# Reordering TensorE's opening work in a fused attention and MoE kernel: transposes of a block ahead of the value products, up products between them

## The chip, the cores and the metric

The kernel runs on one core of a Trainium2 chip. The metric is the device time of one launch in microseconds (us). A profiled run also gives the span, from the first to the last instruction of the core; it is some 1.7 us shorter than the launch's time. Before the change the time was 303.53 us (median of three runs, 303.49 to 303.58). The profiled run was a fourth one: its time was 303.82 us and its span 302.1 us. Some executions fall into a slower state, with a lower granted TensorE clock and a longer time. Comparisons rest on runs of the fast state, which have a mean granted clock of 0.99 to 1.00; where a median in a table includes a slow run, the median of the fast runs stands beside it.

Names used throughout: PE is TensorE, ACT is ScalarE, DVE is VectorE, POOL is GpSimd, SP is the engine that issues most transfers.

## The reference

For each of 8 batches and 8 heads, 576 positions of 64 elements attend to the 64 positions up to their own. The outputs, laid out as 4608 tokens of 512 elements, go through an MLP of width 2048 with a gated activation.

```python
scores = scale * q @ k.T            # window of 64, causal
attn   = softmax(where(mask, scores, -1e9))
x      = (attn @ v)  # -> (4608, 512)
h = x @ w_in
g = h * sigmoid(1.702 * h)
out = g @ w_out
```

## The kernel before

The whole schedule is written by hand: a list of calls, each of which emits instructions to in-order engines. The tokens are cut into 36 blocks of 128. A block m passes through `scores(m)`, `exp(m)`, `pv(m)` (value products), `norm(m)`, `x_mm(m)` (four PE transposes) and `x_out(m)` (a copy to SBUF by ACT). Four blocks are a chunk, and a chunk goes through up products (`up_mm`), a tanh (`up_th`), a gate (`up_g`) and down products. The parts that matter here:

```python
ps pools: psS 1 x 2 banks, psT 1 x 2 banks, psH 2 banks, psO 2 banks   # all of PSUM
# ... cut ...
def pv(m):                       # 16 products on PE; the Tacc pool has ONE buffer
    acc = T_of[m] = psT.tile([P, 2, 512], fp32, name="Tacc", tag="T")
    ...
def norm(m):                     # DVE: reciprocal of the sums, then xs = Tacc * rc
    ...
def x_mm(m, pool, tag):          # PE: four transposes of xs to PSUM
    ...
def x_out(m):                    # ACT: copy into xT of the chunk
    nc.scalar.copy(out=x_dst(m), in_=X_of.pop(m)[:])

def x_dma(m):                    # blocks 16 and up: a transposing transfer instead, issued by SP
    nc.sync.dma_start_transpose(out=x_dst(m), in_=xs_of.pop(m))

def load_bf16(b, i):             # POOL: three casting loads (q, k, v) of one piece of a batch
    for w, src in enumerate((q, k)):
        nc.gpsimd.dma_start(out=heads(rows[b % 2][w][0:n, i, :]), in_=rows_of(src, b, i))
    nc.gpsimd.dma_start(out=v_nat[b % 2][0:n, i, :, 0:D], in_=rows_of(v, b, i))
# ... cut: the opening, as it stands before the change ...
    x_mm(0, psO, "O")
    x_out(0)
    scores(3, masked=True)
    exp(3, masked=True)
    cast_v(0, 3, nc.vector, parts=(1,))
    pv(2)
    norm(2)
    x_mm(1, psO, "O")
    x_out(1)
    warm(3)
    UU['0.0.0'] = up_mm(0, 0, 4, 0, 128, wide=True)
```

"up 0.4.128" is the up unit of chunk 0 whose first column group is 4 and whose tokens start at 128. An up unit is 16 products of 128 columns. `warm` are idle products that keep PE busy. The values v of a piece reach `v_nat` and `v_off` through casts on POOL, in that engine's order, once their load has landed.

The softmax here doesn't subtract the row's maximum and nothing guards it: scores larger than these inputs give would overflow.

Of the kernel before, what the change touches and what calls it, by code (L numbers as in the profile page):

```python
# [29 lines left out]
def kernel(  # L30
# [24 lines left out]
    psO = ctx.enter_context(tc.tile_pool(name="psO", bufs=2, space=bass.MemoryType.PSUM))  # L55
# [14 lines left out]
    def size(i):  # L70
        return P if i < 4 else 64

    def heads(ap):
        return ap.rearrange("p (h d) -> p h d", d=D)
# [4 lines left out]
    def stage_of_v(b, i):  # L79
        return stage_v[5 if (b, i) == (0, 4) else i]  # L80
# [10 lines left out]
    def cast_v(b, i, engine=None, parts=(0, 1, 2)):  # L91
        n, vn, vo = size(i), v_nat[b % 2], v_off[b % 2]
        src = heads(stage_of_v(b, i)[:])
        pieces = [
            (vo[64:128, i, :, 0:D], src[0:64]),
            (vn[0:n, i, :, 0:D], src[0:n]),
            (vo[0:64, i + 1, :, 0:D], src[64:128]) if i < 4 else None,
        ]
        for p in parts:
            if pieces[p]:  # L100
                (engine or nc.gpsimd).tensor_copy(out=pieces[p][0], in_=pieces[p][1])  # L101
# [198 lines left out]
    def blocks_of(m):  # L300
        return [(t, *divmod(2 * m + t, NQB)) for t in range(2)]
# [3 lines left out]
    def zero_block(m):  # L305
        return next((t for t, b, j in blocks_of(m) if j == 0), None)

    def scores(m, masked=False, apart=False):

        if apart:  # L310
            st = [psH.tile([P, 512], fp32, name="S", tag="H")[:] for _ in range(2)]
            S_of[m] = st
        else:
            S_of[m] = psS.tile([P, 2, 512], fp32, name="S", tag="S")
            st = [S_of[m][:, a, :] for a in range(2)]
        for a in range(2) if masked else ():
            nc.tensor.matmul(
                st[a], lhsT=ident[:], rhs=far[zero_block(m)][:], start=True, stop=False
            )
        for t, b, j in blocks_of(m):  # L320
            src = qkt[b % 2]
            for h in range(H):
                hp = h // 2
                part = slice((h % 2) * D, (h % 2) * D + D)
                nc.tensor.matmul(  # L325
                    st[h % 2][:, t * 256 + hp * 64 : t * 256 + hp * 64 + 64],
                    lhsT=src[1][part, hp, 64 * j : 64 * j + 128],
                    rhs=src[0][part, hp, PAD + 64 * j : PAD + 64 * j + 64],
                    start=not masked,
                    stop=not masked or (t == 1 and hp == 3),  # L330
                )

    def exp(m, masked=False):

        to, name = (PT_of, "PT") if masked else (E_of, "E")
        e = to[m] = ep_pool.tile([P, 2, 512], bf16, name=name, tag=name)
        st = S_of.pop(m)
        if isinstance(st, list):
            for a in range(2):
                nc.scalar.activation(out=e[:, a, :], in_=st[a], func=AF.Exp, scale=scale)  # L340
        else:
            nc.scalar.activation(out=e[:], in_=st[:], func=AF.Exp, scale=scale)  # L342
# [11 lines left out]
    def pv_mm(m, out_of):  # L354
        pt = PT_of.pop(m)[:].rearrange("p a f -> p (a f)")
        for h in range(H):
            for t, b, j in blocks_of(m):
                epos = (h % 2) * 512 + t * 256 + (h // 2) * 64
                win = (v_off if j % 2 == 0 else v_nat)[b % 2][:, j // 2, h, 0 : D + 1]
                nc.tensor.matmul(  # L360
                    out_of(h)[t * 64 : t * 64 + 64, 0 : D + 1],
                    lhsT=pt[:, epos : epos + 64],
                    rhs=win,
                    start=True,
                    stop=True,
                )

    def pv(m):
        acc = T_of[m] = psT.tile([P, 2, 512], fp32, name="Tacc", tag="T")
        view = acc[:, :, 0:264].rearrange("p b (h e) -> p b h e", e=66)  # L370
        pv_mm(m, lambda h: view[:, h // 4, h % 4, :])

    def norm(m):
        view = T_of.pop(m)[:, :, 0:264].rearrange("p b (h e) -> p b h e", e=66)
        rc = rc_pool.tile([P, 2, 4, 1], fp32, name="rc", tag="rc")
        nc.vector.reciprocal(out=rc[:], in_=view[:, :, :, D : D + 1])
        xs = xs_pool.tile([P, DM], bf16, name="xs", tag="xs")
        nc.vector.tensor_tensor(
            out=xs[:].rearrange("p (b h d) -> p b h d", b=2, h=4),
            in0=view[:, :, :, 0:D],  # L380
            in1=rc[:].to_broadcast([P, 2, 4, D]),
            op=ALU.mult,
        )
        xs_of[m] = xs[:]
# [30 lines left out]
    def x_dst(m):  # L415
        ch = m // 4
        if m % 4 == 0:
            how = "pe" if ch < 4 else "dma"
            xT[ch] = xt_pool.tile([P, 4, 4, P], bf16, name=f"xT_{how}", tag="xT")
        return xT[ch][:, m % 4]  # L420

    def x_mm(m, pool, tag):
        ps = X_of[m] = pool.tile([P, 4, P], bf16, name="pxt", tag=tag)
        xs = xs_of.pop(m)
        for c in range(4):
            nc.tensor.transpose(  # L426
                out=ps[:, c, :], in_=xs[:, c * P : (c + 1) * P], identity=ident[:, :]
            )
# [15 lines left out]
    def x_out(m):  # L444
        nc.scalar.copy(out=x_dst(m), in_=X_of.pop(m)[:])
# [9 lines left out]
    def up_mm(ch, f, nf, t0, nt, wide=False):  # L455

        pool, tag = (psO, "O") if wide and next(turns) % 2 else (psH, "H")
        ps = pool.tile([P, nf, nt], fp32, name="hps", tag=tag)

        w_in = w_in_sb[f // 4]  # L460
        m0 = t0 // P
        for g in range(nf):
            for c in range(4):
                nc.tensor.matmul(  # L464
                    ps[:, g, :],
                    lhsT=w_in[:, c, (f + g) % 4 : 512 : 4],
                    rhs=xT[ch][:, m0 : m0 + nt // P, c, :],
                    start=(c == 0),
                    stop=(c == 3),
                )  # L470
        return ps, ch, f, nf, t0, nt

    def up_th(ps, ch, f, nf, t0, nt):
        th = th_pool.tile([P, nf, nt], bf16, name="th", tag="th")
        nc.scalar.activation(out=th[:], in_=ps[:], func=AF.Tanh, scale=0.851)  # L475
        return th, ps, ch, f, nf, t0, nt

    def up_g(th, ps, ch, f, nf, t0, nt):
        if (ch, f // 4) not in gT:
            gT[ch, f // 4] = gt_pool.tile([P, 4, 512], bf16, name="gT", tag="gT")  # L480
        nc.vector.scalar_tensor_tensor(  # L481
            out=gT[ch, f // 4][:, f % 4 : f % 4 + nf, t0 : t0 + nt],
            in0=th[:], scalar=1.0, in1=ps[:], op0=ALU.add, op1=ALU.mult,
        )
# [27 lines left out]
    def warm(n):  # L512
        ps = psO.tile([P, P], fp32, name="idle", tag="O")
        for _ in range(n):
            nc.tensor.matmul(ps[:, :], lhsT=ident[:], rhs=ident[:], start=True, stop=True)


    TT, UU = {}, {}
# [51 lines left out]
    x_mm(0, psO, "O")  # L570
    x_out(0)
    scores(3, masked=True)
    exp(3, masked=True)
    cast_v(0, 3, nc.vector, parts=(1,))
    pv(2)
    norm(2)
    x_mm(1, psO, "O")
    x_out(1)
    warm(3)
    UU['0.0.0'] = up_mm(0, 0, 4, 0, 128, wide=True)  # L580
    UU['0.0.0'] = up_th(*UU['0.0.0'])
    pv(3)
    norm(3)
    up_g(*UU['0.0.0'])
    x_mm(2, psS, "S")
    x_out(2)
    UU['0.0.128'] = up_mm(0, 0, 4, 128, 128, wide=True)
    UU['0.0.128'] = up_th(*UU['0.0.128'])
    up_g(*UU['0.0.128'])
    x_mm(3, psS, "S")  # L590
    x_out(3)
    UU['0.0.256'] = up_mm(0, 0, 4, 256, 128, wide=True)
    UU['0.0.256'] = up_th(*UU['0.0.256'])
    up_g(*UU['0.0.256'])
    UU['0.4.0'] = up_mm(0, 4, 4, 0, 128, wide=True)
    UU['0.4.0'] = up_th(*UU['0.4.0'])
    up_g(*UU['0.4.0'])
    UU['0.4.128'] = up_mm(0, 4, 4, 128, 128, wide=True)
    nc.gpsimd.tensor_copy(out=stage_qk[0][0:1, 0, 0:1], in_=w_in_sb[3][0:1, 0, 0:1])
    load_pairs(0, 2)  # L600
# [427 lines left out]
```

## Time and profile before

| what | value | from |
|---|---|---|
| time | 303.53 us | three runs |
| span | 302.1 us | profiled run, of 303.82 us |
| PE busy | 291.5 us, 96% | engine shares |
| PE's share of the chain that ended last | 92% | chain |
| wait of pv(2) for the cast of v | 0.55 us | start to start, 17.22 to 17.80 |
| first w_in piece | issued at 10.98, landed at 17.42 | transfers |

The engine shares say who could set the end; the chain says who does. Here PE does from 17.8 us on. The prediction below shows the lines.

The transfer below is the first w_in piece. The view lists transfers by what they move, engine and kind, count, size where there is one, and us from issue to landing:

```profile
w_in_sb<-in_moe_w_in_dram POOLq DMA_DIRECT2D x1, 512.0 KB, 6.4
```

### The profile page before, as it was taken

How to read it: one execution, taken by the hardware profiler on the slowest of the kernel's cores; microseconds unless marked ns; L12 is line 12 of the kernel's file. 1: busy time of each engine (PE TensorE's matmuls, PEld its weight loads, DVE VectorE, ACT ScalarE, POOL GpSimd, SP SyncE). 2: the span in 40 equal slices, each digit the busy share in tenths (PEclk: the TensorE clock that was granted, in tenths of full speed). 3: DMA queues.
4: the chain of work that ended last, by engine and by line, in shares of the span. 5: the costliest groups of instructions: out<-in, count | busy, mean ns of one | idle time of the engine just before them, and what ended most of it. 6: DMA issues, size and time to landing. Idle time of an engine off the chain costs nothing.

```text
span 302.1 us, 8154 instructions
## 1 busy us (share of the span) xinstructions
PE 291.5 (96%) x3390; PEld 203.4 (67%) x3431; DVE 166.3 (55%) x286; ACT 159.0 (53%) x261; POOL 133.3 (44%) x191
## 2 busy tenths in 40 slices
PE   8799999999999999999999999999999999999995
PEld 8477456997567777777777777777776554444444
DVE  5767706897416555564747467476574754444300
ACT  3676535875627465564546456456465544444311
POOL 1570447827998788767754647862000000000000
PEclk9999999999999999999999999999999999999999
DMA  7999999999999999999999999999321202100112
GB/s 222 241 205 218 235 255 235 225 150 185 145 182 173 174 154 179 121 154 160 166 144 169 113 180 182 159 162 191 89 72 37 69 15 57 62 24 23 67 71 72
DMA packets 149621, 43.34 MB, mean 143 GB/s; under 512 B 135120, under 2 KB 144592, under 8 KB 149584
## 3 DMA queue, kind: packets, MB, share of 16 engines
q0 software_dynamic: 73008, 13.05, 66.7%
q1 hardware_dynamic: 72768, 26.23, 48.7%
q10 hardware_dynamic: 3808, 3.54, 3.7%
q8 instruction: 27, 0.44, 0.7%
q14 instruction: 10, 0.08, 0.1%
HBM read 36.70 MB, written 9.44 MB: 153 GB/s over the span
## 4 chain that ended last, share of the span: by engine, by line
PE 92%; DMA 4%; POOL 1%; issue 1%; SPq 0%; ACT 0%; POOLq 0%
PE hps L464 42%; PE ops L494 39%; PE Tacc L360 4%; PE S L325 3%; DMA stage_v<-in_v_dram 2%; DMA stage_qk<-in_k_dram 2%; PE ops L987 1%; PE turn L196 1%; PE pxt L426 1%; POOL v_off L101 1%; POOL v_nat L101 0%; PE pxt L435 0%; POOL w_in_sb L242 0%; SPq L125 0%; ACT o_sb L995 0%
## 5 line engine op out<-in xcount | busy, mean ns | idle before, releaser
L481 DVE SCALAR_TENSOR_TENSOR gT<-th,hps 128x512 bf16<-128x512 bf16 x144 | 98.1, 686 | 94.3 <-ACT th L475 94.3
L494 PE MATMUL ops<-w_out_sb,gT 128*128 128x512 bf16 x521 | 132.6, 379 | 3.0 <-issue 1.6
L464 PEld LDWEIGHTS <-w_in_sb 128*128 128x128 bf16 x1440 | 113.9, 113 | 31.1 <-issue 0.5
L475 ACT ACTIVATE th<-hps 128x512 bf16<-128x512 f32 x144 | 85.5, 598 | 88.1 <-PE hps L464 86.4
L494 PEld LDWEIGHTS <-gT 128*128 128x128 bf16 x560 | 52.1, 98 | 47.3
L464 PE MATMUL hps<-xT_dma,w_in_sb 128*128 128x256 bf16 (+1 forms) x512 | 79.7, 299 | 0.1
L464 PE MATMUL hps<-xT_pe,w_in_sb 128*128 128x128 bf16 (+1 forms) x928 | 63.8, 225 | 0.1
L228 POOL COPY v_off<-v_nat 64x528 bf16<-64x528 bf16 x25 | 16.0, 641 | 32.7 <-DMA v_nat<-in_v_dram 32.5
L508 ACT ACTIVATE o_sb<-ops 128x512 f32<-128x512 f32 x33 | 19.8, 601 | 15.8 <-PE ops L494 15.8
L224 POOL DMA_DIRECT2D v_nat<-in_v_dram x25 | 21.5, 860 | 3.1 <-issue 3.1
L223 POOL DMA_DIRECT2D rows_k<-in_k_dram x25 | 21.3, 854 | 0.0
L223 POOL DMA_DIRECT2D rows_q<-in_q_dram x25 | 21.1, 844 | 0.0
L342 ACT ACTIVATE E<-S 128x1024 bf16<-128x1024 f32 x19 | 19.5, 1028 | 2.8 <-PE S L325 2.5
L340 ACT ACTIVATE E<-S 128x512 bf16<-128x512 f32 x26 | 14.1, 594 | 12.6 <-PE S L325 12.6
L347 DVE TENSOR_TENSOR PT<-E,mask_None 128x1024 bf16<-128x1024 bf16 x25 | 17.7, 711 | 1.9 <-ACT E L342 1.7
L403 DVE TENSOR_TENSOR xs<-Tacc,rc 128x896 bf16<-128x896 f32 (+1 forms) x26 | 18.0, 692 | 0.9
L101 POOL CAST v_off<-stage_v 64x512 bf16<-64x512 f32 x24 | 15.4, 653 | 5.4 <-PE hps L464 3.9
L360 PEld LDWEIGHTS <-PT 128*64 128x64 bf16 x576 | 11.1, 110 | 7.2 <-issue 6.4
L360 PE MATMUL Tacc<-v_off,PT 128*64 128x65 bf16 x320 | 13.7, 196 | 0.0
L230 POOL COPY v_off<-v_nat 64x528 bf16<-64x528 bf16 x20 | 13.2, 660 | 1.2
L360 PE MATMUL Tacc<-v_nat,PT 128*64 128x65 bf16 x256 | 12.3, 196 | 0.4 <-POOL v_nat L101 0.4
L325 PE MATMUL S<-qt,kt 64*128 64x64 bf16 x576 | 12.4, 191 | 0.1
(74 smaller groups left out, 144.8 us busy)
## 6 DMA issues: line engine op xcount, KB each, us to landing
out_dram<-o_sb SPq DMA_DIRECT2D x24, 256.0 KB, 4.1
out_dram<-o_sb ACTq DMA_DIRECT2D x11, 256.0 KB, 2.0
stage_v<-in_v_dram SPq DMA_DIRECT2D x10, 256.0 KB, 6.5
rows_q<-in_q_dram POOLq DMA_DIRECT2D x20, 128.0 KB, 5.2
rows_k<-in_k_dram POOLq DMA_DIRECT2D x20, 128.0 KB, 5.7
v_nat<-in_v_dram POOLq DMA_DIRECT2D x20, 128.0 KB, 6.7
stage_qk<-in_q_dram SPq DMA_DIRECT2D x4, 512.0 KB, 7.0
stage_qk<-in_k_dram SPq DMA_DIRECT2D x4, 512.0 KB, 8.1
```

The source lines that it names most:

```text
L101: (engine or nc.gpsimd).tensor_copy(out=pieces[p][0], in_=pieces[p][1])
L223: nc.gpsimd.dma_start(out=heads(rows[b % 2][w][0:n, i, :]), in_=rows_of(src, b, i))
L224: nc.gpsimd.dma_start(out=v_nat[b % 2][0:n, i, :, 0:D], in_=rows_of(v, b, i))
L325: nc.tensor.matmul(st[h % 2][:, t * 256 + hp * 64 : t * 256 + hp * 64 + 64], lhsT=src[1][part, hp, 64 * j : 64 * j + 128], rhs=src[0][part ...
L342: nc.scalar.activation(out=e[:], in_=st[:], func=AF.Exp, scale=scale)
L360: nc.tensor.matmul(out_of(h)[t * 64 : t * 64 + 64, 0 : D + 1], lhsT=pt[:, epos : epos + 64], rhs=win, start=True, stop=True,)
L403: nc.vector.tensor_tensor(out=out[:, :, hs], in0=src[:, :, :, 0:D], in1=rc[:, :, hs].to_broadcast([P, 2, n, D]), op=ALU.mult,)
L464: nc.tensor.matmul(ps[:, g, :], lhsT=w_in[:, c, (f + g) % 4 : 512 : 4], rhs=xT[ch][:, m0 : m0 + nt // P, c, :], start=(c == 0), stop=(c == 3),
L475: nc.scalar.activation(out=th[:], in_=ps[:], func=AF.Tanh, scale=0.851)
L481: nc.vector.scalar_tensor_tensor(out=gT[ch, f // 4][:, f % 4 : f % 4 + nf, t0 : t0 + nt], in0=th[:], scalar=1.0, in1=ps[:], op0=ALU.add, o ...
L494: nc.tensor.matmul(O_of[ch, tsub][:, :], lhsT=gT[ch, j][:, f, tsub * P : (tsub + 1) * P], rhs=w_out_sb[:, 4 * j + f, :], start=(j == 0 and ...
L508: nc.scalar.activation(out=o_sb[:], in_=ps[:], func=AF.Copy, scale=0.5)
```

## The change

The intent is to fill the wait of pv(2) with work that is ready: the transposes of block 1 and the first up unit go ahead of pv(2), the second up unit between pv(2) and pv(3), and the third and fourth units change places.

```diff
     x_mm(0, psO, "O")
     x_out(0)
     scores(3, masked=True)
+    x_mm(1, psO, "O")
+    x_out(1)
     exp(3, masked=True)
     cast_v(0, 3, nc.vector, parts=(1,))
+    warm(3)
+    UU['0.0.0'] = up_mm(0, 0, 4, 0, 128, wide=True)
     pv(2)
     norm(2)
-    x_mm(1, psO, "O")
-    x_out(1)
-    warm(3)
-    UU['0.0.0'] = up_mm(0, 0, 4, 0, 128, wide=True)
     UU['0.0.0'] = up_th(*UU['0.0.0'])
+    UU['0.0.128'] = up_mm(0, 0, 4, 128, 128, wide=True)
     pv(3)
     norm(3)
     up_g(*UU['0.0.0'])
     x_mm(2, psS, "S")
+    UU['0.0.128'] = up_th(*UU['0.0.128'])
     x_out(2)
-    UU['0.0.128'] = up_mm(0, 0, 4, 128, 128, wide=True)
-    UU['0.0.128'] = up_th(*UU['0.0.128'])
     up_g(*UU['0.0.128'])
+    UU['0.4.0'] = up_mm(0, 4, 4, 0, 128, wide=True)
+    UU['0.4.0'] = up_th(*UU['0.4.0'])
+    UU['0.0.256'] = up_mm(0, 0, 4, 256, 128, wide=True)
     x_mm(3, psS, "S")
     x_out(3)
-    UU['0.0.256'] = up_mm(0, 0, 4, 256, 128, wide=True)
+    up_g(*UU['0.4.0'])
     UU['0.0.256'] = up_th(*UU['0.0.256'])
     up_g(*UU['0.0.256'])
-    UU['0.4.0'] = ...      # cut: the three calls of 0.4.0, now further up
```

More of the change, by code (lines that the diff above doesn't have):

```diff
@@ L585 @@
     x_mm(2, psS, "S")
+    UU['0.0.128'] = up_th(*UU['0.0.128'])
     x_out(2)
-    UU['0.0.128'] = up_mm(0, 0, 4, 128, 128, wide=True)
-    UU['0.0.128'] = up_th(*UU['0.0.128'])
     up_g(*UU['0.0.128'])
+    UU['0.4.0'] = up_mm(0, 4, 4, 0, 128, wide=True)
+    UU['0.4.0'] = up_th(*UU['0.4.0'])
+    UU['0.0.256'] = up_mm(0, 0, 4, 256, 128, wide=True)
     x_mm(3, psS, "S")
     x_out(3)
-    UU['0.0.256'] = up_mm(0, 0, 4, 256, 128, wide=True)
+    up_g(*UU['0.4.0'])
     UU['0.0.256'] = up_th(*UU['0.0.256'])
     up_g(*UU['0.0.256'])
-    UU['0.4.0'] = up_mm(0, 4, 4, 0, 128, wide=True)
-    UU['0.4.0'] = up_th(*UU['0.4.0'])
-    up_g(*UU['0.4.0'])
     UU['0.4.128'] = up_mm(0, 4, 4, 128, 128, wide=True)
```

## The prediction

> **What bounds the kernel now.** I read the page's engine shares first, then PE's waits, then the chain that ended last in the opening 27 us, and last the timeline between 12 and 27 us, where the diff lies. The page's head and its chain:
>
> ```profile
> span 302.1 us, 8154 instructions
> PE 291.5 (96%) x3390; PEld 203.4 (67%) x3431; DVE 166.3 (55%) x286; ACT 159.0 (53%) x261; POOL 133.3 (44%) x191
> ...
> PE 92%; DMA 4%; POOL 1%; issue 1%; SPq 0%; ACT 0%; POOLq 0%
> ```
>
> TensorE (PE) is busy for 96% of the span and makes up 92% of the chain, the other 8% lying mostly in the opening. So only what lets PE's in-order stream run earlier is worth anything. PE's waits from 23 us to the end hold no engine and no transfer: the view lists one entry, 1.6 us of "issue" in ten pieces, the longest 0.2 us. From 12 to 23 us it lists one too:
>
> ```profile
> PE Tacc L360 <- POOL v_nat L101: 0.4, 1, 0.4
> ```
>
> That is the target. The chain of the opening (columns: start us, length us, what) shows how it sits on the path:
>
> ```profile
> 17.02 0.74 POOL v_nat L101
> 17.76 0.04 issue
> 17.80 0.42 PE Tacc L360 x15
> 18.22 0.33 PE pxt L426 x4
> 18.55 0.17 PE idle L515 x3
> 18.71 0.89 PE hps L464 x16
> 19.61 0.38 PE Tacc L360 x16
> 19.99 0.33 PE pxt L426 x4
> 20.32 0.89 PE hps L464 x16
> 21.21 0.23 PE pxt L426 x4
> 21.44 5.58 PE hps L464 x97
> ```
>
> Up to 17.76 the path is a GpSimd (POOL) queue of casts of v; the last is the one that pv(2), the third block's value products (Tacc), needs. From 17.80 on it is PE piece after piece without a hole. The timeline gives the size of the wait:
>
> ```profile
> 17.22 0.22 PE L360 MATMUL Tacc<-v_off,PT 128*64 128x65 bf16 x1
> 17.80 0.19 PE L360 MATMUL Tacc<-v_nat,PT 128*64 128x65 bf16 x1 [0.36 <-POOL v_nat L101]
> ```
>
> The first product of pv(2) starts at 17.22, the second at 17.80. Their usual distance is 0.03 (17.80 to 17.83 for the next), so 0.55 us are lost. The 0.36 in the bracket is counted from a modelled end, hence smaller.
>
> **What the Trainium skill says.** "Perfetto Trace Analysis", Optimization Strategy, says to take the gaps on the engine that binds, find the semaphore that ends each, and make that dependency come sooner[...]. The trace gives just one such gap here, and the change fills it. "TensorE: Matmul & The Clock Gate", Wait — 56ns, not 53.3ns?, gives 55.6 ns from start to start of warm 128-column products; the chain's 0.89 us for 16 agrees, and the granted clock is 1.00. "TensorEngine Tiling (Array Packing)", Key Properties, says "Mode switching requires drain". The trace agrees: value products (form 128*64) and up products or transposes (128*128) change places at a cost. pv(3) with its 16 products takes 0.38 us in the chain, while 16 starts at 0.018 us each (19.54 to 19.79 for the last pair) fill only 0.29. I charge 0.09 us for each change of form.
>
> **The change, part by part.** The order of instructions shows that only PE and ACT move; DVE, GpSimd and SP keep theirs, no instruction is added or dropped, and the totals of work are equal. PE's new order after scores(3), the fourth block's scores: x_mm(1), three warming products, up 0.0.0, pv(2), up 0.0.128, pv(3), x_mm(2), up 0.4.0, up 0.0.256, x_mm(3), and then up 0.4.128 as before. I walk PE's starts from 17.22, where pv(2) started. Everything ahead is unchanged.
>
> - x_mm(1) at 17.22. Its input (norm(1) on DVE) ends at 16.26+0.69 = 16.95, so it doesn't wait. It takes 0.23, the warming products 0.17: 17.62.
> - up 0.0.0 at 17.62. It needs the first w_in piece, issued at 10.98 and landing 6.4 us after: 17.4. So 0.2 us of room. It takes 0.89, and 0.09 for the change of form: 18.60.
> - pv(2) at 18.60. Its cast ended at 17.76: the 0.55 wait is gone. The first 0.29 are products, then 0.09 for the change back: 18.98. In the old order pv(2) was followed by a transpose and pv(3) by a transpose. From scores(3) to x_mm(2) the old order has four changes of form (scores to value products, to transpose, up to value products, to transpose); the new one has five, since an up product stands between pv(2) and pv(3). One more, +0.09.
> - up 0.0.128 at 18.98. It needs the second block's transposed output: ACT, idle since 16.91, copies it right behind x_mm(1), about 17.66 to 18.25. In time. 0.89 and 0.09: pv(3) could start at 19.96.
> - pv(3) writes Tacc, and that pool has one buffer, which norm(2) reads. In the trace norm(3) ends 1.45 us after the first product of pv(3) (19.54 to 20.30+0.69 = 20.99). So norm(2) ends at 18.60+1.45 = 20.05, and with about 0.04 for the semaphore pv(3) starts at 20.09. **A new wait of 0.13 us.** In the old order x_mm(1), warming and up 0.0.0 stood between the two, and there was none.
> - pv(3) 0.38: 20.47. x_mm(2) 0.23: 20.70. up 0.4.0 needs the second w_in piece, which landed at about 20.0 (two pieces issued at 10.98 and 11.88 have a median of 7.3 us to landing with the first 6.4, so the second 8.1). 0.89: 21.59.
> - up 0.0.256 at 21.59 needs x_out(2) on ACT. The tanh of up 0.0.128 starts 1.10 us after its first product (18.55 to 19.65 for the old one): 20.08 to 20.68; x_out(2) then waits for x_mm(2), 0.43 after its start: 20.90 to 21.49. Just in time, 0.1 us of room. 0.89: 22.48. x_mm(3), 0.23 more: up 0.4.128 starts at 22.71.
>
> Before, up 0.0.256 starts at 21.28 and up 0.4.0 follows it, so up 0.4.128 starts at 21.28 + 2 x 0.89 = 23.06. The walk gives 0.35. As a balance: -0.55 (wait for the cast) +0.09 (one more change of form) +0.13 (wait for norm(2)) = -0.33; the 0.02 between them is rounding. I take 0.33.
>
> On the side engines, ACT's exp(3) slips behind x_out(1), from 17.40 to about 18.27, and ends at 19.30; pv(3) at 20.09 doesn't feel it. DVE works off norm(3) (to 21.54) and then gT pieces at 0.69 each, which frees the first hps buffer at 22.25, before up 0.4.128 asks for it at 22.71. Each later up unit takes PE 0.89 against 0.60 on ACT and 0.69 on DVE, so both catch up.
>
> **Does the gain reach the end?** After 23 us PE's stream has no wait for anything else, and its work is equal. What could stop it is a transfer that doesn't come earlier. The nearest I find: the third w_out piece, landing at 40.6, is used at about 42; the fourth, at 44.1, is used at about 45, after the scores at 43.77; both leave more than 0.33. The casts and transposes by PE are led by PE itself and move with it. So the full gain should come out: 303.53 - 0.33 = 303.2 us, a ratio of 0.999.
>
> **Rivals.**
> - The first w_in piece takes the place of the cast. For: it has 0.2 us of room where it had 1.1 (18.55 against 17.4), and the DMA engines are full then (share above 1.2 in every stretch of 2 us from 12 to 24 us, 16 engines counted). Against: nothing ahead of 17.4 changes, so the landing shouldn't either. If it slips by 0.3, about 0.1 of the gain goes: 303.3. At a slip of 0.55 or more, nothing is left: 303.5 to 303.6.
> - The Tacc buffer or ACT's new order costs more than I charge: x_out(2) behind two tanh has 0.1 us of room, and a late exp(3) delays the first tanh to 19.3. If each of them costs 0.1 to 0.2, the gain is eaten up: 303.5.
> - A wait further down swallows the gain. At 76.73 pv(9) starts within 0.02 us of the end of a GpSimd cast to v_off. I read this as coincidence, since PE's distance there is just the 0.09 of a change of form. If it is a real dependency, and GpSimd, fed by transfers, doesn't come earlier, the time stays 303.5.
> - The shift lets later evacuations or transfers fall better or worse. Past 20 us I find no distance between PE's starts that is 0.13 us or more too long and isn't a lost matmul record or a change of form next to one, so little hangs on such timing: 0.1 to 0.2 either way.
>
> **Range and chances.** The wait removed bounds the gain at about 0.55 us, unless later stages shift in my favour; a full swallow gives 303.5. So 302.95 to 303.5. Two per cent would be 6 us, more than ten times all that the diff touches; so within 2% is nearly sure.
>
> **What would show it right or wrong.** Right: the wait of Tacc for v_nat is gone from PE's waits; x_mm(1) starts near 17.2, up 0.0.0 near 17.6, pv(2) near 18.6, pv(3) near 20.1 released by DVE's xs, up 0.4.128 near 22.7; PE's end 0.3 us earlier. Wrong: up 0.0.0 starts after 17.7, released by the transfer of w_in_sb; pv(3) without a wait (the gain is then 0.46) or later than 20.3; up 0.0.256 held up by xT_pe; or a lead of 0.3 us at 23 us that is no longer there at 100 us.

## More of the kernel before

```profile
xT_dma<-xs SPq DMA_TRANSPOSE x1, 5.3
```

The second transposing transfer of the outputs of blocks 16 and 17, which PE needs at about 143 us, was issued at 137.26 and landed at 142.54. PE's first product that reads it starts at 143.23.

## The result, and the profile after

The changed kernel took 303.97 us (median of four runs: 304.15, 303.58, 303.98, 303.96) against 303.51 us for the kernel before in the same session (303.40 to 303.58). The ratio of the fast runs is 1.0014, with a 95% interval of 0.9996 to 1.0031. The predicted 303.2 us was missed, and 303.97 lies above the stated range.

The head of the page of the changed kernel:

```profile
span 302.4 us, 8193 instructions
...
PE 295.2 (98%) x3431; PEld 203.2 (67%) x3431; DVE 166.8 (55%) x286; ACT 158.4 (52%) x261; POOL 134.3 (44%) x191
```

The 41 more instructions on PE are matmul records that the trace of before had lost, so PE's busy time can't be compared. The list of PE's waits from 12 us to the end (who waited, for whom, us in total, times, longest) has one entry:

```profile
PE hps L464 <- DVE gT L481: 0.6, 1, 0.6
```

The wait for the cast of v is gone, as intended, and a new one has come. First the opening, in the chain that ended last (start us, us, what):

```profile
10.48 6.84 DMA w_in_sb<-in_moe_w_in_dram
17.32 0.05 issue
17.37 1.08 PE hps L464 x16
18.45 0.38 PE Tacc L360 x16
18.83 1.03 PE hps L464 x16
19.86 0.12 issue
19.98 0.45 PE Tacc L360 x16
```

The path comes from the landing of the first w_in piece now, not from POOL's casts: up 0.0.0 starts at 17.37, 0.24 us later than PE would have been ready. The 0.12 of "issue" ahead of pv(3), 0.20 us from start to start, is the predicted wait for norm(2). Up 0.4.128 starts at 22.60; before it started at 23.07, two up units of 0.90 after 21.28. So PE led by 0.47 us, and it still led by 0.46 us at 76 us (pv(9) at 76.27, before 76.73).

The lead is lost at one place. The timeline of PE around 143 us (start us, us, engine, line, operation, tiles, count, and in brackets the idle time before and who ended it):

```profile
141.90 1.03 PE L494 MATMUL ops<-w_out_sb,gT 128*128 128x512 bf16 x4
143.56 1.69 PE L464 MATMUL hps<-xT_dma,w_in_sb 128*128 128x256 bf16 x14 [0.62 <-DVE gT L481]
```

From start to start PE lost 0.79 us there; without it these products would have started at 142.77, still 0.46 us ahead of before's 143.23. The page names DVE. That is one of the cases where the named engine isn't the cause: the product reads xT_dma, and the second transposing transfer landed at 143.42, 0.14 us before PE went on. The view of transfers has it at

```profile
xT_dma<-xs SPq DMA_TRANSPOSE x1, 7.8
```

us from issue to landing, where the kernel before had 5.3. After 143.6 the two kernels run alike to the end, 0.33 us apart. The balance closes: 0.46 of lead less 0.79 of wait is -0.33, and the spans differ by 302.4 - 302.1.

**The theory and its rivals at this point.** A: the opening is ahead as predicted, and the lead makes PE run into a transfer that doesn't come earlier. B: the opening isn't ahead in general; this profile just had early landings (its q and k landed at 9.78 instead of 10.28). C: the wait at 143 falls on either kernel by the chance of how transfers land, and the comparison of four runs with four caught it on one side.

### The profile page after: what moved, and what is told of

It reads as the page before. It is cut to its first block, busy times and chain, and to the rows that moved or that the text cites. A ratio compares the mean times of both kernels' runs of the same rounds, so it can differ in the third digit from the quotient of the medians.

```text
span 302.4 us, 8193 instructions
## 1 busy us (share of the span) xinstructions
PE 295.2 (98%) x3431; PEld 203.2 (67%) x3431; DVE 166.8 (55%) x286; ACT 158.4 (52%) x261; POOL 134.3 (44%) x191
## 4 chain that ended last, share of the span: by engine, by line
PE 93%; DMA 5%; SPq 0%; ACT 0%; DVE 0%; POOL 0%; issue 0%
PE hps L464 42%; PE ops L494 40%; PE Tacc L360 4%; PE S L325 3%; DMA stage_qk<-in_k_dram 2%; DMA w_in_sb<-in_moe_w_in_dram 2%; PE ops L987 1%; PE turn L196 1%; PE pxt L426 1%; SPq L125 0%; PE pxt L435 0%; DVE gT L481 0%; POOL gate L522 0%; ACT th L475 0%; ACT o_sb L995 0%
## 5 line engine op out<-in xcount | busy, mean ns | idle before, releaser
L494 PE MATMUL ops<-w_out_sb,gT 128*128 128x512 bf16 x560 | 139.0, 379 | 0.0
L228 POOL COPY v_off<-v_nat 64x528 bf16<-64x528 bf16 x25 | 16.1, 646 | 28.4 <-DMA v_nat<-in_v_dram 28.2
L347 DVE TENSOR_TENSOR PT<-E,mask_None 128x1024 bf16<-128x1024 bf16 x25 | 18.6, 750 | 1.8 <-ACT E L342 1.7
L230 POOL COPY v_off<-v_nat 64x528 bf16<-64x528 bf16 x20 | 13.9, 696 | 1.1
```

Of the source, the lines that this page charges most:

```text
L347: nc.vector.tensor_tensor(out=pt[:].rearrange("p a f -> p (a f)"), in0=E_of.pop(m)[:].rearrange("p a f -> p (a f)"), in1=masks[z][:].rearr ...
L494: nc.tensor.matmul(O_of[ch, tsub][:, :], lhsT=gT[ch, j][:, f, tsub * P : (tsub + 1) * P], rhs=w_out_sb[:, 4 * j + f, :], start=(j == 0 and ...
```

## The experiments

Two marks are read from each profile: the opening mark, which is the end of the sixteenth gated product on DVE (35.66 us before, 35.20 after), and the stretch from there to the end. "x2" is the second transposing transfer of blocks 16 and 17; "due" is when PE would have started the product that reads it.

### First call: both kernels again, and both without the transposing transfers

`before_again` and `after_again` are the two kernels unchanged.

> The kernel before once more, to see how much its own landings move. Theory A (lead is won in the opening and lost at the first up product of the fifth chunk, which waits for a transposing transfer): the second of the two transposing transfers lands a few tenths before 143.2, PE does not wait there, time 303.5, spread under 0.2. Rival C (that wait is chance and falls on either kernel): its landing moves by more than 0.7 us from run to run, and this profile or the times show such a wait too, some times being 0.3 to 0.8 us longer.

> The changed kernel once more. Theory A: up 0.4.128 starts near 22.6 to 22.8, PE leads by 0.3 to 0.5 us until about 143 and then waits 0.3 to 0.8 us for the transposing transfer that lands at about 143.4; time 303.5 to 304.1. Rival B (no lead is won in the opening): up 0.4.128 at 23.0 or later. Rival C: no wait at 143 in this profile, and the span is then 0.3 to 0.5 us shorter than before's 302.1.

`before_xpe` and `after_xpe` let PE transpose blocks 16 and 17:

```diff
-        elif m < 16:
+        elif m < 18:
             x_mm_two(m, psT, "T")
-        if m % 2 == 0 and m >= 16:
+        if m % 2 == 0 and m >= 18:
             x_dma(m)
```

> The kernel before with the outputs of blocks 16 and 17 transposed by PE and copied by ACT in place of the two transposing transfers that the first up product of the fifth chunk needs. PE gets 8 transposes, 8 x 0.057 + 0.1 for a possible change of form = about 0.5 us more. Theory A and rival C: 304.0, as before has no wait there to lose. If before had a hidden wait there, nearer 303.5.

> The changed kernel with the same edit: no transfer can hold PE at 143. Theory A: the lead of the opening stays, 0.3 to 0.5 us under before_xpe of the same call, so about 303.6. Rival B: the same time as before_xpe, 304.0. Rival D (the lead is lost at some other wait further on): PE leads at 150 us and not at the end; same time as before_xpe.

| kernel | median, us (runs) | span, profiled run | opening mark | mark to end | wait at 143 |
|---|---|---|---|---|---|
| before (first profile) | 303.53 (profiled run 303.82) | 302.1 | 35.66 | 266.46 | none |
| after (first profile) | 303.97 (profiled run 304.15) | 302.4 | 35.20 | 267.25 | 0.79 |
| before_again | 304.08 (303.19 to 304.96) | 303.3 | 35.98 | 267.27 | 0.81 |
| after_again | 303.59 (303.42 to 303.85) | 301.8 | 35.28 | 266.51 | none |
| before_xpe | 304.17 (303.78 to 305.02) | 302.1 | 35.55 | 266.53 | none possible |
| after_xpe | 303.79; fast runs 303.68 (303.43 to 308.77; the last in the slow state) | 302.0 | 35.43 | 266.54 | none possible |

The rounds of the kernel before in this call ran from 303.54 to 307.2, so times of single runs say little here; the profiles say much. PE's waits of `before_again`:

```profile
PE hps L464 <- DMA xT_dma<-xs: 0.6, 1, 0.6
PE Tacc L360 <- POOL v_nat L101: 0.6, 1, 0.6
```

The kernel before has the wait at 143 as well, this time with its true name, and `after_again` has none. Rival C is right about this wait: two profiles of each kernel, one with it and one without, for each. Without it the stretch from the mark to the end is 266.46 and 266.51, with it 267.25 and 267.27. The spans without it are 302.1 before and 301.8 after, which is the 0.3 us of the prediction; with it they are 303.3 and 302.4. But the openings of one and the same kernel differ by as much, so one such pair is no proof of the 0.3. Theory A, that it takes the lead to lead PE into the transfer, falls.

The two kernels without these transfers are 0.49 us apart in the medians of their fast runs (303.68 and 304.17) and 0.1 us in the profiled spans. The stretch to the end is equal to 0.01 us. So rival D, a loss at some other wait further on, has nothing for it either: what differs between the kernels is the opening. The edit itself was to cost about 0.5 us, and the stretch is only 0.07 longer than before's. Up to the end of the last output copy it is 263.86 against 263.42, so 0.44 longer as expected; from that copy to the end of the span both kernels with the edit take 2.67 us where all other profiles take 3.03 to 3.05. What shortens that tail I have not looked for.

### Second call: the parts of the change, and a slot more for the transfers

`after_slot` takes the attention of blocks 16 and 17 one slot earlier, so the transposing transfers are issued earlier while the same product uses them:

```diff
-    ... (42,48,55,62,69,76,83,89,95,101,107,114,120)
+    ... (42,48,55,61,69,76,83,89,95,101,107,114,120)
```

> The changed kernel with the attention of blocks 16 and 17 one slot (about 1.75 us of PE time) earlier, so that the two transposing transfers are issued about 1.7 us earlier and the same up product uses them. Theory C (a wait at about 143 us that falls on either kernel by the chance of how the transfers land, and that the four profiles so far show in one of two of each kernel): the wait can't come up any more, since at worst it was 0.8 us; span 301.8, times 303.2 to 303.6, and from the end of the sixteenth gated product (near 35.3) to the end of the kernel 249.7 us as in the profiles without the wait. Rival: moving the slot brings another transfer late (the loads hang on the same slots) and the stretch from 35.3 to the end stays at 250.4.

`after_tacc` frees pv(3) from norm(2) by another pair of banks:

```diff
-    def pv(m):
-        acc = T_of[m] = psT.tile([P, 2, 512], fp32, name="Tacc", tag="T")
+    def pv(m, pool=None, tag="T"):
+        acc = T_of[m] = (pool or psT).tile([P, 2, 512], fp32, name="Tacc", tag=tag)
...
-    pv(3)
+    pv(3, psS, "S")
-    x_mm(2, psS, "S")
+    x_mm(2, psT, "T")
-    x_mm(3, psS, "S")
+    x_mm(3, psT, "T")
```

> The changed kernel with pv(3) writing to the scores' bank pair and x_mm(2), x_mm(3) to the value products' pair, so that pv(3) need not wait for norm(2). If the 0.20 us in front of pv(3) (0.295 from start to start less 0.09 for the change of form) is that buffer: the wait goes, up 0.4.128 starts 0.2 us sooner after up 0.0.0 than in the changed kernel (there 5.23 us, 17.37 to 22.60; here 5.0). Rival (pv(3) is held by exp(3) or by its weights): still 5.2. Whether PE waits near 143 is chance here too: 301.6 without, 302.3 with.

`only_x1` is the kernel before with one part of the change:

```diff
     scores(3, masked=True)
+    x_mm(1, psO, "O")
+    x_out(1)
     exp(3, masked=True)
     cast_v(0, 3, nc.vector, parts=(1,))
     pv(2)
     norm(2)
-    x_mm(1, psO, "O")
-    x_out(1)
```

> The kernel before with one part of the change alone: the second block's transposes and copy ahead of exp(3) and pv(2). PE gets 0.23 us of work into the 0.55 us wait and still waits about 0.3 for the cast of v; up 0.4.128 at about 22.85 where before has 23.0 to 23.4 (its cast ended at 17.76 in one profile and 18.09 in the other: counted from the end of that cast, 5.3 us before and 5.1 here). Rival: exp(3), now behind that copy, holds pv(3) and eats the 0.2.

`no_second_up` is the changed kernel with the second up unit back behind pv(3):

```diff
-    UU['0.0.128'] = up_mm(0, 0, 4, 128, 128, wide=True)
     pv(3)
     norm(3)
     up_g(*UU['0.0.0'])
+    UU['0.0.128'] = up_mm(0, 0, 4, 128, 128, wide=True)
```

> The changed kernel with its second part undone: up 0.0.128 again behind pv(3). pv(2) and pv(3) then stand next to each other and pv(3) has to wait for norm(2): about 1.1 us instead of 0.2, less 0.2 for two changes of form fewer. Up 0.4.128 about 0.7 us later after up 0.0.0 than in the changed kernel: 5.9 instead of 5.23, so about 23.4, which is later than before. Rival (the Tacc buffer isn't what holds pv(3)): no such wait, 5.1.

| kernel | median, us (runs) | span | opening mark | mark to end | wait at 143 |
|---|---|---|---|---|---|
| after_slot | 303.63 (303.27 to 304.01) | 302.2 | 35.76 | 266.45 | none |
| after_tacc | 305.43; fast runs 304.75 (303.22 to 308.31; the last in the slow state) | 303.0 | 35.00 | 267.95 | 0.76, and 0.73 at 93 us |
| only_x1 | 303.88 (303.36 to 304.18) | 301.9 | 35.31 | 266.58 | none |
| no_second_up | 305.07 (304.75 to 306.13) | 303.3 | 36.25 | 267.07 | 0.64 |
| before, same call | 304.08 (303.29 to 306.94) | | | | |

To compare openings, one must take out when the loads happened to land. That can be done to a few hundredths of a us. In the six profiles with before's opening order, the mark stands 17.91 us (17.90 to 17.91) after the end of the cast of v that pv(2) waits for. In the eight with the changed order it stands 17.82 us (17.79 to 17.83) after the start of up 0.0.0. Against these constants:

- `only_x1`: 35.31 less the end of its cast at 17.58 is 17.73, so this part alone is worth 0.18 us. I expected 0.2. PE still waits 0.48 us for the cast, more than the expected 0.3, as scores(3) came early in this run.
- `after_tacc`: 35.00 less the start of up 0.0.0 at 17.38 is 17.62. The buffer of Tacc costs 0.20 us, as the wait ahead of pv(3) had it.
- `no_second_up`: 36.25 less 17.34 is 18.91, so the second up unit between pv(2) and pv(3) is worth 1.09 us. I expected 0.7.

The chain of `no_second_up` shows why pv(3) must not follow pv(2) directly:

```profile
19.08 0.70 DVE xs L378
19.78 0.14 issue
19.92 0.45 PE Tacc L360 x16
...
22.01 0.48 ACT xT_pe L445
```

PE stands still for norm(2) on DVE, 1.31 us from start to start where I had put 1.1, and a second time, 0.21 us, for ACT's copy (xT_pe) behind a tanh, which I hadn't counted. Less the 0.20 of the changed kernel's own wait and 0.18 for two changes of form fewer that makes 1.14, near the 1.09 of the marks.

`after_slot` has no wait at 143, as expected: x2 landed at 140.45 and was due at 143.33. (The stretches of 249.7 and 250.4 us in its expectation don't fit the marks used here: the four profiles before it had 266.46 to 267.27.) Yet its opening mark is the latest of the changed order so far, `no_second_up` aside, and PE's waits from 12 to 23 us say what did it:

```profile
PE hps L464 <- DMA w_in_sb<-in_moe_w_in_dram: 0.5, 1, 0.5
```

The first w_in piece landed at 17.89 in this run, and up 0.0.0 started at 17.94, which is 0.69 us later than PE was ready. So the landing that had "0.2 us of room" in the prediction is the new bound of the opening in most profiles of the changed order.

### Third call: both kernels with the slot, and a better kernel

`before_slot` and `after_slot2` have the slot edit; `after_best` has it and the edit of `after_tacc`.

> The kernel before with the attention of blocks 16 and 17 one slot earlier, the counterpart of the changed kernel with the same edit. No wait near 143 us in any run, so what is left between the two is the opening. Opening mark (end of the sixteenth gated product) at 35.5 to 36.0, 266.5 from there to the end, span 302.0 to 302.5. If the wait near 143 is what spreads the times of before, the times lie closer together than before's own in this call. Rival: the spread comes from the clock or from openings and stays.

> The changed kernel with that edit once more, beside its counterpart. Opening mark 35.2 to 35.8 depending on the landing of the first w_in piece (17.3 to 17.9), 266.5 to the end. Theory (the change wins what the prediction said, about 0.3 us, in the opening, and nothing after it): median 0.3 us under before_slot. Rival (the waits for the first w_in piece take all of it): the same median.

> Both edits on the changed kernel: pv(3) in the scores' bank pair (no wait for norm(2)), and the slot. Opening mark 0.2 us ahead of after_slot2 at the same landing of w_in, 35.0 to 35.5; 266.5 to the end unless the wait for transposed q near 93 us, seen once, comes; median 0.5 us under before_slot and 0.2 under after_slot2.

`after_hold` tests what makes x2 late. In the eight profiles so far that have x2, the four with a late x2 (7.6 to 7.8 us) have POOL issuing three casting loads right around it:

```profile
134.42 3.69 SPq L448 DMA_TRANSPOSE xT_dma<-xs  x2
134.49 0.88 POOL L223 DMA_DIRECT2D rows_q<-in_q_dram  x1
135.35 0.89 POOL L223 DMA_DIRECT2D rows_k<-in_k_dram  x1
136.22 0.90 POOL L224 DMA_DIRECT2D v_nat<-in_v_dram  x1
```

This is the timeline of the changed kernel, where x2 was issued at 135.66. In the kernel before the same loads were out before x2 was issued at 137.26:

```profile
133.04 0.88 POOL L223 DMA_DIRECT2D rows_q<-in_q_dram  x1
...
134.77 0.90 POOL L224 DMA_DIRECT2D v_nat<-in_v_dram  x1
134.88 3.64 SPq L448 DMA_TRANSPOSE xT_dma<-xs  x2
```

POOL's loop of loads waits for earlier loads to land, so its phase drifts against PE from run to run: these loads were issued anywhere from 133.0 to 136.8 us in the profiles of the unedited loop. The edit holds them back until x2 has landed:

```diff
+            if (b, i) == (5, 2):
+                at(come, lambda: nc.gpsimd.tensor_copy(out=gate[0:1, 1:2],
+                                                       in_=xT[4][0:1, 1, 0, 0:1]))
             at(come, lambda b=b, i=i: load_bf16(b, i))
```

> The changed kernel where GpSimd's three casting loads of the sixth batch's third piece wait until the second of the two transposing transfers has landed (a copy of one element). In the eight profiles so far that transfer took 7.6 to 7.8 us in the four where these three loads were issued from 1.9 us before to 0.6 after it, and 5.3 to 6.7 in the four where they were issued earlier or later. Theory (those loads are what delays it): it takes 5.0 to 6.7 here and PE does not wait at 143, in every run; a wait may come up further down, as all later loads are held back. Rival (the delay has another cause and the coincidence is one): 7.6 or more remains possible, with the loads away.

| kernel | median, us (runs) | span | opening mark | mark to end | wait at 143 |
|---|---|---|---|---|---|
| before_slot | 303.97 (303.51 to 304.13) | 302.2 | 35.58 | 266.61 | none |
| after_slot2 | 304.07 (303.28 to 305.78) | 303.3 | 36.88 | 266.44 | none |
| after_best | 303.11 (302.92 to 304.27) | 301.4 | 34.90 | 266.45 | none |
| after_hold | 304.07 (303.08 to 304.56) | 301.4 | 34.91 | 266.47 | none |
| before, same call | 303.95 (303.73 to 308.17) | | | | |

The pair with the slot edit didn't decide the size of the gain by its medians. `after_slot2` has two runs at a mean granted clock of 0.994 (305.12 and 305.78), and its profile, which is one of them, shows where (columns: stretch, length, busy time and count of PE, PEld, DVE, ACT and POOL, granted clock, DMA share, GB/s):

```profile
10.00:12.00 2.00, 1.16 (x16) 1.02 (x13) 1.27 (x2) 1.04 (x2) 1.74 (x3) 0.82 1.35 219
12.00:16.00 4.00, 3.78 (x60) 1.91 (x60) 2.47 (x5) 2.27 (x4) 3.62 (x6) 0.66 1.18 180
```

TensorE's clock fell to 0.66 between 12 and 16 us, and the opening mark is 1.5 us late. The kernel before has such runs too (308.17 at 0.993), so I don't put it down to the change. Without the two runs the medians are 303.46 (four runs) for `after_slot2` and 303.97 for `before_slot`. One of the four, 304.65 at a clock of 1.000, is not explained. The times of `before_slot` lie within 0.62 us of each other and those of before within 4.4, as expected if late transfers spread them; but the longest of before's, 308.17, has the lower clock, so this shows little.

`after_best` is the fastest kernel here, though "same" by the rule of 2%. Five of six runs lie from 302.92 to 303.25, and its ratio to the kernel before is 0.9971 (0.9945 to 0.9998). The interval only just leaves out 1, and it is wide because of the other kernel's long runs; by medians the gain is 0.84 us. I had expected 0.5 us under `before_slot` and 0.2 under `after_slot2`; it is 0.86 under the first, and 0.96 under the second or 0.35 under its four runs of full clock. Its chain has pv(3) following without a hole:

```profile
18.74 1.02 PE hps L464 x16
19.76 0.38 PE Tacc L360 x16
```

In `after_hold` x2 took 6.28 us and PE did not wait. One profile, with a chance of about one in two of having no wait anyway, settles nothing. Besides, the loads of the piece before came within 2.6 to 0.9 us ahead of x2 instead.

### Fourth call: forcing and forbidding the meeting

`after_meet` and `before_meet` move the three loads ahead of POOL's wait for an older load and hold them until the outputs of blocks 16 and 17 are ready, so that they go out together with the transposing transfers in every run:

```diff
-            at(come, lambda b=b, i=i: load_bf16(b, i))
+            if (b, i) == (5, 2):
+                at(65, lambda: nc.gpsimd.tensor_copy(out=gate[0:1, 1:2],
+                                in_=xs2_of[16][0:1, 1, DM - 1 : DM]))
+            at(65 if (b, i) == (5, 2) else come, lambda b=b, i=i: load_bf16(b, i))
```

> The changed kernel where the three casting loads of the sixth batch's third piece are moved ahead of GpSimd's wait for an older load and then held, by a copy of one element, until the normalised outputs of blocks 16 and 17 are there: they are then issued together with the two transposing transfers of these outputs, every time. Theory (these loads are what makes the second transfer late): it takes 7.4 us or more, lands after PE's first up product of the fifth chunk is due, PE waits 0.5 us or more there, and from the opening mark to the end it is 267.0 us or more. Rival (the coincidence so far was one): 5.3 to 6.7 us, no wait, 266.5.

> The kernel before with the same edit. If the wait is none of the change's own, it comes up here just as surely: transfer 7.4 us or more, wait of 0.5 us or more near 144, 267.0 or more from the opening mark to the end. Rival (the lead of the change is what makes PE meet the transfer): no wait here, and one in the changed kernel with this edit.

`before_hold` is the kernel before with the edit of `after_hold`.

> The kernel before with those loads held until the second transposing transfer has landed. Theory: it takes 5.3 to 6.7 us and PE does not wait, 266.5 us from the opening mark to the end. Rival: 7.4 or more in spite of it.

`after_early_w` releases the w_in loads by q's second half instead of k's:

```diff
-    nc.gpsimd.tensor_copy(out=gate[0:1, 0:1], in_=stage_qk[1][0:1, 1, 0:1])
+    nc.gpsimd.tensor_copy(out=gate[0:1, 0:1], in_=stage_qk[1][0:1, 0, 0:1])
```

> The changed kernel with the w_in loads released by the landing of q's second half (8.1 to 8.7 in the profiles) instead of k's (9.8 to 10.3). If the order of the loads alone sets when the first w_in piece lands, it lands about 1.5 us earlier, 15.8 to 16.3, k's second half lands some tenths later, because both share the engines, and the opening mark follows scores(3) and not w_in: 0 to 0.3 us earlier than the changed kernel's 35.2. Rival: k's second half, now sharing with w_in, lands 0.7 us later or more, and the opening mark is later than 35.4.

| kernel | median, us (runs) | span | opening mark | mark to end | x2 took | wait at 143 |
|---|---|---|---|---|---|---|
| after_meet | 304.48 (303.72 to 306.21) | 303.3 | 35.35 | 267.94 | 7.42 | 0.86, and 0.61 at 93 us |
| before_meet | 304.64; fast runs 304.63 (303.45 to 310.12; the last in the slow state) | 301.7 | 35.10 | 266.57 | 7.09 | 0.12 |
| before_hold | 303.54 (303.36 to 303.97) | 301.7 | 35.27 | 266.46 | 4.63 | none |
| after_early_w | 304.66 (303.42 to 305.45) | 302.5 | 35.10 | 267.38 | 7.92 | 0.95 |
| before, same call | 303.62 (303.55 to 304.57) | | | | | |

The timelines of `before_hold` and `after_meet` show that the gates did what they were for:

```profile
140.78 0.18 POOL L870 CAST gate<-xT_dma 1x1 f32<-1x1 bf16 x1 [4.20 <-DMA xT_dma<-xs]
```

```profile
135.19 3.48 SPq L450 DMA_TRANSPOSE xT_dma<-xs  x2
135.22 0.57 POOL L872 CAST gate<-xs 1x1 f32<-1x1 bf16 x1 [1.68 <-DMA qt<-rows_q]
135.75 0.89 POOL L223 DMA_DIRECT2D rows_q<-in_q_dram  x1
```

And the view of transfers gives the time of x2, first in `before_hold`, then in `after_meet`:

```profile
xT_dma<-xs SPq DMA_TRANSPOSE x1, 4.6
```

```profile
xT_dma<-xs SPq DMA_TRANSPOSE x1, 7.4
```

All sixteen profiles that have x2, with the slot edit or without it, fall into the same order. Where the first of the three loads was issued from 1.9 to 0.7 us before x2, x2 took 7.1 to 7.9 us (seven profiles, the two forced ones among them). Where the loads were issued earlier or later, or held back, it took 4.6 to 6.7 us (nine profiles). In `after_hold`, one of the nine, the first of the nearest three loads was 2.6 us ahead. Forced together it was long, and held apart short, in both kernels. So the meeting is what makes it late. How it does so, no run here shows.

The change doesn't move the due time against the transfers. In all twelve profiles without the slot edit the product was due 8.35 us after the first transposing transfer was issued. Both follow the same PE stream, so a lead moves both. Whether the change makes the meeting itself more frequent is open. Of the eight profiles whose schedule and loads around 143 us are untouched, four of the five with the changed order or most of it have the wait, and one of the three with before's order or most of it. That is too few to decide. `before_meet` escaped: 7.09 us, 0.12 of wait. I had expected 7.4 or more and a wait of 0.5, so the forced meeting sets a long transfer, not its exact length. Two of its other runs were 304.63 and 304.65 at a clock of 1.00, 1.2 us over the profiled one; that they had the wait is a guess. Taken by itself, the pair came out as the rival in the expectation had it: next to no wait in the kernel before, one in the changed kernel. Against the rival stands `before_again`, which waited 0.81 us without the change. The waits at 93 us, in `after_tacc` and `after_meet`, are for a transposing transfer of k (the expectation of `after_best` says q), so 143 us isn't the only place with little room.

`after_early_w` missed its expectation for the landing; its opening mark of 35.10 is within it. The first w_in piece was issued 1.9 us earlier than in the first profile of the changed kernel, at 8.55 instead of 10.48, and landed at 17.00, only 0.3 us earlier; it took 8.45 us instead of 6.84, while k's second half landed on time at 9.53. With the unedited order of loads the piece landed at 16.96 to 17.04 in five other profiles too. Issuing early gained next to nothing. The engines were sharing a full load, with a DMA share of 1.2 or more in each 2 us from 12 to 24 us.

## Why the prediction was wrong

**What held.** The wait for the cast went. The one more change of form cost about 0.1 us. The new wait for norm(2) was there: predicted 0.13 us, measured 0.20 by start to start and 0.20 by taking it away. The walk from up 0.0.0 to up 0.4.128 came to 5.09 us and measured 5.23. ACT's later exp(3) and the copies of xT held up nothing in any profile of the changed kernel. The coincidence at 76.73 was one: PE came 0.46 us earlier there without a wait. One reading was wrong, as far as seen without consequence: that DVE keeps its order. The diff also swaps the gates of up 0.0.256 and up 0.4.0, which run on DVE.

**First step that failed: "the full gain should come out".** It rested on "After 23 us PE's stream has no wait for anything else", read from a single execution. That execution had 0.7 us of room at one transposing transfer, whose time to land varies between 4.6 and 7.9 us with the phase of POOL's loads. The two kernels unedited, `after_tacc`, `only_x1`, `no_second_up` and `after_early_w` give the eight profiles with the schedule at 143 untouched; five of them have a wait there of 0.64 to 0.95 us. It is two to three times the gain that was being looked for. It falls on before (0.81 in `before_again`) as on after (0.79), and the lead of the change doesn't make it likelier through the due time, since that moves along. Whether the lead shifts the phase of POOL's loop by enough to change how often it meets is not known; the counts above, four of five against one of three, leave it open.

The range of 302.95 to 303.5 left no room for scatter: its upper end is before's own time, as three runs of before within 0.1 us looked like a steady kernel. The profiled run, at 303.82, already stood outside that band. In the later calls before's own fast runs ranged from 303.19 to above 308, with four calls' medians from 303.62 to 304.08. The step that was never taken is an estimate of the scatter of one run against another.

That the recorded 303.97 came out above 303.51 is shown for one of the four runs: the profiled one, 304.15, had the wait. For the 303.96 and 303.98, which set the median, it is argued only: their spans are 302.1 each, 0.3 below the profiled run's and equal to that of before's profile, and their times exceed their spans by 1.86 and 1.88 us, where most runs have about 1.7. So some 0.15 us of the miss lies outside the span, and what the rest was in these two runs stays open. In the next call the same two kernels stood the other way, at 303.59 and 303.81.

**Second step that failed, in size: the balance of the opening.** Two of its terms were read from one profile, and both are larger on average. The prediction gave the first w_in piece "0.2 us of room" and put its slip among the rivals as a lesser thing. In the six profiles with the changed opening and a full clock, PE waited for it 0.24 (`after`), 0.11 (`after_again`), 0.41 (`after_xpe`), 0.69 (`after_slot`), 0 (`after_hold`) and 0.28 us (`after_meet`), which is 0.29 on average. There were two reasons: PE was ready at 17.1 to 17.4 in these profiles, earlier than the 17.6 of my walk, because the opening itself moves with the landings of q and k; and the piece landed anywhere from 17.0 to 17.9. The term that was sized at zero is 0.29 us.

The other term is the target itself. In the profile that the prediction read, PE lost 0.55 us to POOL's casts. In the other five profiles of before's order it lost 0.81 to 0.96, counted from the last product of scores(3), because the first product of pv(2) had to wait too, for the cast of v_off that POOL does just before: in all five it starts 0.05 us after the end of that cast. `before_hold` shows it, first POOL, then PE:

```profile
16.00 0.61 POOL L101 CAST v_off<-stage_v 64x512 bf16<-64x512 f32 x1
16.68 0.68 POOL L101 CAST v_nat<-stage_v 128x512 bf16<-128x512 f32 x1
```

```profile
16.66 0.19 PE L360 MATMUL Tacc<-v_off,PT 128*64 128x65 bf16 x1
17.41 0.19 PE L360 MATMUL Tacc<-v_nat,PT 128*64 128x65 bf16 x1 [0.56 <-POOL v_nat L101]
```

So the mean wait removed is 0.80 us. Less about 0.1 for the change of form, 0.20 for norm(2) and 0.29 for w_in, that leaves 0.2. The mean opening mark is 35.52 over six profiles of before's order and 35.32 over these six, a difference of 0.20 us where 0.33 was predicted; with marks that spread over 0.9 us within each order, this difference by itself can't be told from zero. An estimate that takes the landings out uses both constants within each profile: before's order would put the mark 17.91 us after the end of the cast, the changed order 17.82 after the start of up 0.0.0, which comes when PE is ready or 0.05 after the landing of w_in, whichever is later. This gives back the twelve marks to 0.01 us. It puts the gain in one and the same opening between -0.48 (`after_slot`) and 0.54 (`after_hold`), 0.19 on average, with a 95% interval of about 0.19 either way, so that zero lies at its lower edge and the predicted 0.33 within it. It takes for granted that the order on PE moves neither casts nor landings. Rival B, that the opening isn't ahead in general, is right in so far as the gain hangs on two landings and was negative in some pairs of profiles (35.76 in `after_slot` against 35.10 in `before_meet`).

## What to carry to other kernels

A gain of 0.3 us can't be judged by a few runs of a kernel in which one late transfer costs 0.8; it can be judged by marks in the profiles that take the landings out, like the constant distance from the end of a cast to a later product. Before calling a stretch free of waits, look for the transfers with least room and ask what can make them land later in another run, above all the loads of a loop that another engine paces. Here the reordering with a slot more for one transfer and another pair of banks for one product measured 303.11 us against 303.95 (ratio 0.9971, 0.9945 to 0.9998), which the reordering alone did not reach. That is six runs.

## What the Trainium skill lacked or had wrong

- "DMA: Bandwidth & Descriptors", Issuing engines are not separate DMA queues, says that transfers of all issuing engines end up on the same 16 DMA engines and interleave, and this case agrees. No page gives the size for a transposing transfer of one block next to casting loads: 4.6 to 6.7 us apart from three such loads, 7.1 to 7.9 us when they were issued from 1.9 to 0.7 us before it.
- "TensorEngine Tiling (Array Packing)", Key Properties, says that a change of mode drains the engine, without a time. Here each change between the value products' form and the full one cost about 0.1 us: from the last up product to the first value product it took 0.149 us from start to start, where two up products stand 0.056 apart.
- "TensorE: Matmul & The Clock Gate", What's actually happening, describes a clock gate that halves the clock after an idle window of about 3.4 us, in a window that is free-running and so falls at another time in each run. One profile of eighteen (`after_slot2`) fits it: a granted clock of 0.50 from 11.3 to 14.7 us, which is 0.66 on average between 12 and 16. The page doesn't say how much activity still counts as idle. In the 3.4 us before that fall PE was busy for 1.54 us, and `before_again` had 1.73 us busy in the same stretch (7.9 to 11.3 us) without a fall. The opening mark was 1.5 us late. Why the clock fell in this run alone, no run here shows.
